# Pooled attention and a gated MLP on one core: the 288-column operands of four more products are read from two quarters in turn

## The chip, the core and the metric

The kernel runs on one core of a Trainium2 chip. The core's engines are TensorE (PE, with its weight loads shown apart as PEld), VectorE (DVE), ScalarE (ACT), GpSimd (POOL) and SyncE (SP), which issues nearly all DMA transfers here. The metric is the device time of one execution in microseconds, taken as the median of several runs. A trace of one further execution, with start and duration of every instruction, is what the rows below are read from.

## The reference

For 8 batches of 576 positions, 8 heads of 64, all fp32:

```python
k_p = k.reshape(B, H, Sp, 8, D).mean(axis=3)         # pooled by 8: Sp = 72
v_p = v.reshape(B, H, Sp, 8, D).mean(axis=3)
attn = softmax(q @ k_p.T / sqrt(D))
x = (attn @ v_p), heads side by side                 # (B, 576, 512)
h = gelu_tanh(x @ w_in)                              # w_in 512 x 1024
u, v = h[..., :512], h[..., 512:]
v_n = (v - mean(v)) / sqrt(var(v) + 1e-6) * g_ln
v_s = einsum('ts,bsd->btd', w_sg, v_n) + b_sg[None, :, None]   # w_sg 576 x 576
out = x + (u * v_s) @ w_out                          # w_out 512 x 512
```

## The kernel before

The program is a long list of small steps. `ORDER`, a list written out in the code, says which step of which batch comes next (`H0+2` is step H, part 0, two batches on), and a last loop pins the order on every engine to it, so each engine works through a fixed queue. Eight batches are interleaved in this way; a batch takes some 60 us.

Most products are "rounded": an fp32 operand is split into a high part that is rounded to fp32r and a low part with the remainder (`wih` and `wil`, `xhl` with both parts of x, `wsh`/`wsl`, `vhh`/`vhl`, `ghi`/`glo`, `woh`/`wol`, `vbh`/`vbl`, `ah`/`al`), and three fp32r matmuls (high by high, high by low, low by high) stand for one fp32 product. The positions (576) lie along the free dimension, in SBUF as one row of 576 floats in a partition. [...] 

The steps that matter here, each for one of four blocks of 128 output rows (features):

- **V**: attention weights times pooled values, x of one block. From batch 3 on (`BY_HEAD` holds 0, 1, 2) it is a rounded product of 8 matmuls per block, 288 columns each, read from `ah`, `al` and `lt`. For batches 0 to 2 it is plain fp32 on 64-wide tiles. Then PSUM is read back three times: `h` (rounded high part into `xhl`), `x` (plain copy into `x32`) and `rest` (the low part). Which engine does each of these is set by the table `OTHER`; `rest` reads PSUM on VectorE, or else `x32` on GpSimd.
- **H** (and **J**, its form for batch 0): the v half of h, positions on the partitions, 512 features as columns, 12 matmuls of 512 columns for each block of positions. Here the moving operand is already read through `woven`: column 0 from the first half, column 1 from the second, column 2 from the first again.
- **U**: the u half of h, 24 matmuls of 288 columns for each block; ScalarE reads PSUM through the gelu into `u`.
- **W**: the product with w_sg, 28 matmuls of 288 columns for each block; VectorE scales by `g_ln` and adds `b_sg` (`bbc`) in PSUM, then multiplies by `u`.
- **O**: the product with w_out, 24 matmuls of 288 columns for each block; VectorE adds it to `x32`.
- **S**, **T**, **D**, **K**, **P**: scores and softmax, transposes, dummy matmuls at the start, and pooling. They issue fp32 matmuls, which the trace shows as two records each.

`woven` is `x.rearrange("p (a b) -> p b a", a=2)`: of n columns, the first and the second half in turn. All matmuls are issued by the helper `mm` (L143).

Of the kernel before, what the change touches and what calls it, by code (L numbers as in the profile page):

```python
# [13 lines left out]
AF = mybir.ActivationFunctionType  # L14
ALU = mybir.AluOpType
AX = mybir.AxisListType

P = 128
# [6 lines left out]
BY_HEAD = (0, 1, 2)  # L25
# [70 lines left out]
def tile_pooled_attn_gmlp(ctx: ExitStack, tc: tile.TileContext, q, k0, kv0, v0, k, v, vleft, w_in, w_sg, bg, w_out, out):  # L96
    nc = tc.nc
    B, _, _, S = q.shape
# [7 lines left out]
    KC = DM // P  # L106
    NT = -(-S // P)
    TAIL = S - (NT - 1) * P
    HALF = S // 2
# [26 lines left out]
    def atile():  # L136
        return ring(psa, [P, 2, NB], "aps", 2)

    def woven(x):
        return x.rearrange("p (a b) -> p b a", a=2)  # L140

    def mm(o, lhsT, rhs, start, stop):
        nc.tensor.matmul(o, lhsT, rhs, start=start, stop=stop)  # L143

# [35 lines left out]
    vbh = const.tile([P, G, P], F32R, name="vbh")  # L180
    vbl = const.tile([P, G, P], F32R, name="vbl")
# [23 lines left out]
    st = {}  # L205
# [9 lines left out]
    def copy(o, i, key):  # L215
        if key in OTHER:
            nc.vector.tensor_copy(o, i)
        else:
            nc.scalar.copy(o, i)  # L219
# [9 lines left out]

    def rest(lo, x, ps, hi, key):  # L230
        if key in OTHER:
            nc.vector.tensor_tensor(lo.rearrange("p (a n) -> p a n", a=2), ps,
                                    hi.rearrange("p (a n) -> p a n", a=2), op=ALU.subtract)
        else:
            nc.gpsimd.tensor_tensor(lo, x, hi, op=ALU.subtract)  # L235

# [357 lines left out]
    def step_V(b, g):  # L594
        ah, al = st.pop(("a", b, g))
        lt, vl = st.get(("lt", b, g // 2)), st.get(("vl", b))
        gl = 2 * (g % 2)
        ps = atile()
        for n in range(2):
            sl = slice(HALF * n, HALF * (n + 1))  # L600
            o = ps[:, n, 0:HALF]
            if b in BY_HEAD:
                for h, (w, x) in enumerate(((st["vp", b][0:SP, g], ah), (st["vo", b][:, g], al))):
                    mm(o[D * h:D * h + D], w, x[:, sl], True, True)
                continue
            mm(o, vbh[:, g], ah[:, sl], True, False)
            mm(o, vbl[:, g], ah[:, sl], False, False)
            mm(o, vl[:, g // 2, gl:gl + 2], lt[:, sl], False, False)
            mm(o, vbh[:, g], al[:, sl], False, True)
        yield  # L610
        if ("x32", b) not in st:
            st["x32", b] = dbl.tile([P, KC, S], F32, name="x32")
            st["xhl", b] = (per.tile([P, 2, KC, S], F32R, name="xhl", tag="xhl"),
                            per.tile([P, KC, 2, TAIL], F32R, name="xta"))
        x32, (xhl, xta) = st["x32", b][:, g], st["xhl", b]
        xs, hi = ps[:, :, 0:HALF], xhl[:, 0, g].rearrange("p (a n) -> p a n", a=2)
        copy(hi, xs, f"h{min(b, 3)}{g}")
        copy(x32.rearrange("p (a n) -> p a n", a=2), xs, f"x{min(b, 3)}{g}")
        yield
        rest(xhl[:, 1, g], x32, xs, xhl[:, 0, g].bitcast(F32), f"V{min(b, 3)}{g}")  # L620
        yield
        move(xta[:, g], xhl[:, :, g, S - TAIL:S].bitcast(F32), f"X{min(b, 3)}{g}")
# [72 lines left out]
    def halves(ps, pairs, first, last):  # L695
        for j, (w, x) in enumerate(pairs):
            for n in range(2):
                mm(ps[:, n, 0:HALF], w, x[:, HALF * n:HALF * (n + 1)], first and j == 0, last and j == len(pairs) - 1)

    def step_U(b, d):  # L700
        xhl = st["xhl", b][0]
        xhi, xlo = xhl[:, 0], xhl[:, 1]
        ps = mtile()
        sl = slice(d * P, (d + 1) * P)
        for c in range(KC):
            halves(ps, [(wih[:, c, sl], xhi[:, c]), (wih[:, c, sl], xlo[:, c]), (wil[:, c, sl], xhi[:, c])],
                   c == 0, c == KC - 1)
        yield
        u = per.tile([P, 2, HALF], F32, name="u", tag=f"u{d}")
        ready(AF.Gelu_apprx_tanh)  # L710
        nc.scalar.activation(u, ps[:, :, 0:HALF], AF.Gelu_apprx_tanh)
        st["u", b, d] = u

    def step_W(b, d):
        vhh, vhl, vht = st["vh", b]
        ps = mtile()
        sl = slice(d * P, (d + 1) * P)
        for c in range(NT - 1):
            halves(ps, [(vhh[:, c, sl], wsh[:, c]), (vhh[:, c, sl], wsl[:, c]), (vhl[:, c, sl], wsh[:, c])],
                   c == 0, False)  # L720
        halves(ps, [(vht[:, sl], wth), (vht[:, sl], wtl)], False, True)
        yield
        u = st.pop(("u", b, d))
        vs = ps[:, :, 0:HALF]
        nc.vector.scalar_tensor_tensor(vs, vs, gcol[:, d:d + 1],  # L725
                                       bbc.rearrange("p (a n) -> p a n", a=2), op0=ALU.mult, op1=ALU.add)
        nc.vector.tensor_tensor(u, vs, u, op=ALU.mult)
        yield
        if ("g", b) not in st:
            st["g", b] = (per.tile([P, KC, S], F32R, name="ghi", tag="ghi"),  # L730
                          per.tile([P, KC, S], F32R, name="glo", tag="glo"))
        ghi, glo = st["g", b]
        uf = u.rearrange("p a n -> p (a n)")
        copy(ghi[:, d], uf, f"G{min(b, 2)}{d}")
        yield
        combine(glo[:, d], uf, ghi[:, d].bitcast(F32), ALU.subtract, f"W{min(b, 2)}{d}")

    def step_O(b, m):
        ghi, glo = st["g", b]
        sl = slice(m * P, (m + 1) * P)  # L740
        x = st["x32", b][:, m].rearrange("p (a n) -> p a n", a=2)
        if b == B - 1 and m == G - 1:
            for n in range(2):
                t = slice(HALF * n, HALF * (n + 1))
                ps = (atile, mtile)[n]()[:, 0, 0:HALF]
                for c in range(KC):
                    for j, (w, z) in enumerate([(woh, ghi), (wol, ghi), (woh, glo)]):
                        mm(ps, w[:, c, sl], z[:, c, t], c == 0 and j == 0, c == KC - 1 and j == 2)
                yield
                nc.vector.tensor_tensor(x[:, n], ps, x[:, n], op=ALU.add)  # L750
                yield
            return
        ps = atile() if b == B - 1 and m % 2 else mtile()

        def part(cs):
            for c in cs:
                halves(ps, [(woh[:, c, sl], ghi[:, c]), (wol[:, c, sl], ghi[:, c]), (woh[:, c, sl], glo[:, c])],
                       c == 0, c == KC - 1)
        part(range(KC - 1))
        yield  # L760
        part([KC - 1])
        yield
        nc.vector.tensor_tensor(x, ps[:, :, 0:HALF], x, op=ALU.add)

    def step_Z(b, m):
        x = st["x32", b][:, m]
# [42 lines left out]
    last = {}  # L809
# [11 lines left out]
def _laid_out(inputs):  # L821

    import numpy as np

    a = {n: np.asarray(x) for n, x in inputs.items()}
    B, H, S, D = a["q"].shape
    G, SP, NT = H // 2, S // POOL, -(-S // P)
    q = a["q"].reshape(B, G, 2, S, D).transpose(0, 1, 2, 4, 3).reshape(B, G, 2 * D, S)
    at = [128 * min(r, 2) + 160 * max(r - 2, 0) + 32 * i + j
          for i in range(NT) for r in range(2 * (i == NT - 1), 4) for j in range(32)]  # L830
    a["q"] = np.stack([q[b] if b == 0 else q[b][:, :, at] for b in range(B)])
    n = P * (S // P)
    run = [t for lo, hi in ((0, 384), (448, 576), (384, 448)) for t in range(lo, hi)]
    kt = a["k"][0].reshape(G, 2, S, D).transpose(2, 0, 1, 3).reshape(S, G, 2 * D)[run]
    vt = a["v"][0].reshape(G, 2, S, D).transpose(2, 1, 0, 3).reshape(S, H * D)[run]
    a["k0"] = kt[:n].reshape(S // P, P, G, 2 * D).transpose(1, 2, 0, 3)
    a["v0"] = vt[:n].reshape(S // P, P, H * D).transpose(1, 0, 2)
    a["kv0"] = np.concatenate([kt[n:].reshape(S - n, H * D), vt[n:]])
    a["k"] = a["k"][1:].reshape(B - 1, G, 2, SP, POOL, D).transpose(0, 2, 5, 1, 3, 4).reshape(B - 1, 2 * D, G, SP, POOL)
    v = a["v"][1:].reshape(B - 1, G, 2 * SP, POOL, D).transpose(0, 1, 2, 4, 3)  # L840
    a["v"] = v[:, :, 0:P].transpose(0, 2, 1, 3, 4)
    a["vleft"] = v[:, :, P:].reshape(B - 1, G * (2 * SP - P), D, POOL)
    w = a["moe_w_in"]
    half = w.shape[1] // 2
    a["moe_w_in"] = np.concatenate([w[:, :half], w[:, half::2], w[:, half + 1::2]], axis=1)
    a["moe_w_sg"] = np.concatenate([a["moe_w_sg"].T, a["moe_w_sg"].T[n:]])
    a["bg"] = np.concatenate([np.broadcast_to(a["moe_b_sg"], (P, S)), a["moe_g_ln"].reshape(-1, P).T], axis=1)
    return a


# [19 lines left out]
```

## Time and profile before

| | |
|---|---|
| Time, median of 3 runs | 528.98 us (528.08 to 529.0) |
| The profiled execution's own time | 528.84 us |
| Its span, first to last instruction | 527.1 us |
| PE busy | 517.7 us, 98% of the span |
| DVE busy | 376.2 us, 71% |
| ACT busy | 258.3 us, 49% |
| POOL busy | 240.7 us, 46% |
| Granted TensorE clock, mean over the span | 0.999 of full speed |

Busy times are sums of instruction durations without overlap. A matmul's row has a duration that runs on behind the start of the next one, so the time that a matmul costs the engine is read from the distance between starts, not from its duration.

### The profile page before, as it was taken

Reading aid. Unit: us, or ns where it says so; the run is one execution under the profiler, and the core shown is the slowest. Engines: PE = TensorE matmul, PEld = TensorE weight load, DVE = VectorE, ACT = ScalarE, POOL = GpSimd, SP = SyncE. Lnnn points to the kernel's source line nnn. Section 1 sums busy time; section 2 is a strip of 40 time slices with the busy share of each in tenths; the row PEclk is TensorE's granted clock in tenths of the full one; section 3 lists DMA queues with packets and bytes.
Section 4 is the critical chain, followed back from the end, with each engine's and each line's share of the span. In section 5 each row is a group of like instructions: output and inputs, shape, how many; then the busy total and the mean of one; then the engine's idle time right before and its main releaser. Section 6 shows DMA issues by size and latency. Waiting matters only on the chain.

```text
span 527.1 us, 9508 instructions
## 1 busy us (share of the span) xinstructions
PE 517.7 (98%) x3594; PEld 489.9 (93%) x3594; DVE 376.2 (71%) x593; ACT 258.3 (49%) x510; POOL 240.7 (46%) x333
## 2 busy tenths in 40 slices
PE   8889999999999999999999999999999999999997
PEld 8658899899989999999999999999999999999997
DVE  1789999668857886887679769877749765642362
ACT  2888871586336554485703577274253743142000
POOL 4797664553455629183335615754134741261010
PEclk9999999999999999999999999999999999999999
DMA  8995125837461563056432632344431224000002
GB/s 282 406 347 188 59 68 124 238 110 231 109 176 67 158 224 93 24 153 197 148 98 79 180 96 88 112 110 111 151 125 24 90 68 114 24 22 24 24 2 112
DMA packets 42810, 66.64 MB, mean 126 GB/s; under 512 B 5532, under 2 KB 22028, under 8 KB 42764
## 3 DMA queue, kind: packets, MB, share of 16 engines
q1 hardware_dynamic: 42476, 65.59, 40.6%
q8 instruction: 28, 0.46, 0.4%
q10 hardware_dynamic: 288, 0.44, 0.2%
q14 instruction: 18, 0.15, 0.1%
HBM read 47.14 MB, written 18.73 MB: 125 GB/s over the span
## 4 chain that ended last, share of the span: by engine, by line
PE 92%; ACT 3%; DVE 2%; POOL 2%; issue 0%; POOLq 0%; ACTq 0%
PE mps L143 77%; PE aps L143 15%; ACT e L472 1%; POOL e L458 1%; DVE nmax L506 0%; PE aps L190 0%; POOL rstd L482 0%; DVE e L463 0%; ACT vg L491 0%; DVE glo L228 0%; ACT e L468 0%; POOL glo L228 0%; ACT ah L219 0%; ACT L212 0%; ACT vhh L219 0%
## 5 line engine op out<-in xcount | busy, mean ns | idle before, releaser
L143 PE MATMUL mps<-xhl,wih 128*128 128x288 f32 x512 | 88.7, 295 | 0.3 <-ACT vg L671 0.3
L143 PE MATMUL mps<-wih,xhl 128*128 128x512 f32 x256 | 77.7, 383 | 0.0
L143 PEld LDWEIGHTS mps<-xhl,wih 128*128 128x128 f32 x512 | 75.2, 188 | 1.3 <-ACT vg L671 0.5
L458 POOL TENSOR_TENSOR e<-e,ssum 128x720 f32<-128x720 f32 x29 | 42.1, 1455 | 58.4 <-DVE ssum L457 49.0
L235 POOL TENSOR_TENSOR xhl<-x,xhl 128x576 fp32r<-128x576 f32 x22 | 31.3, 1433 | 53.4 <-ACT x L219 34.2
L143 PE MATMUL mps<-wsh,vhh 128*128 128x288 f32 x256 | 54.8, 295 | 0.0
L143 PE MATMUL mps<-wsl,vhh 128*128 128x288 f32 x256 | 54.7, 295 | 0.0
L143 PE MATMUL mps<-wsh,vhl 128*128 128x288 f32 x256 | 54.7, 295 | 0.0
L143 PE MATMUL mps<-xhl,wil 128*128 128x288 f32 x256 | 54.6, 294 | 0.0
L143 PEld LDWEIGHTS mps<-wih,xhl 128*128 128x128 f32 x256 | 48.1, 189 | 6.4
L143 PE MATMUL mps<-ghi,woh 128*128 128x288 f32 x244 | 53.2, 298 | 0.0
L143 PE MATMUL mps<-glo,woh 128*128 128x288 f32 x244 | 52.4, 294 | 0.0
L143 PE MATMUL mps<-ghi,wol 128*128 128x288 f32 x244 | 52.3, 294 | 0.0
L725 DVE SCALAR_TENSOR_TENSOR mps<-mps,both 128x576 f32<-128x576 f32 x32 | 26.1, 814 | 34.8 <-PE mps L143 34.4
L143 PE MATMUL mps<-wil,xhl 128*128 128x512 f32 x128 | 46.5, 379 | 0.0
L481 POOL TENSOR_TENSOR rstd<-mv,eps 128x1 f32<-128x1 f32 (+1 forms) x40 | 10.3, 258 | 76.8 <-DVE mv L676 76.5
L228 POOL TENSOR_TENSOR glo<-u,ghi 128x576 fp32r<-128x576 f32 x18 | 25.7, 1428 | 41.3 <-ACT ghi L219 23.9
L143 PE MATMUL aps<-kbd,qT 128*128 128x144 f32 x300 | 41.7, 288 | 1.9 <-ACT ah L219 1.2
L143 PEld LDWEIGHTS aps<-kbd,qT 128*128 128x128 f32 x300 | 39.0, 190 | 4.8 <-ACT ah L219 1.4
L143 PEld LDWEIGHTS mps<-wsh,vhh 128*128 128x128 f32 x256 | 41.1, 188 | 0.4 <-issue 0.4
L143 PEld LDWEIGHTS mps<-wsh,vhl 128*128 128x128 f32 x256 | 41.1, 188 | 0.2 <-DVE vhl L228 0.2
L143 PEld LDWEIGHTS mps<-xhl,wil 128*128 128x128 f32 x256 | 40.9, 188 | 0.0
(182 smaller groups left out, 1236.0 us busy)
## 6 DMA issues: line engine op xcount, KB each, us to landing
qT<-in_q SPq DMA_DIRECT2D x31, 288.0 KB
out<-x SPq DMA_DIRECT2D x31, 288.0 KB
kraw<-in_k SPq DMA_DIRECT2D x14, 576.0 KB
vraw<-in_v SPq DMA_DIRECT2D x14, 512.0 KB
al<-tfar SPq DMA_DIRECT2D x20, 288.0 KB
tfar<-y SPq DMA_DIRECT2D x56, 80.0 KB
raw<-in_moe_w_in SPq DMA_DIRECT2D x4, 1024.0 KB
tfar<-y SPq DMA_DIRECT2D x56, 64.0 KB
```

The source lines that it names most:

```text
L143: nc.tensor.matmul(o, lhsT, rhs, start=start, stop=stop)
L228: (nc.vector if key in OTHER else nc.gpsimd).tensor_tensor(o, x, y, op=op)
L235: nc.gpsimd.tensor_tensor(lo, x, hi, op=ALU.subtract)
L458: (nc.gpsimd if key in OTHER else nc.vector).tensor_tensor(e, e, rec.unsqueeze(3).broadcast_to([P, NT, 2, SP]), op=ALU.mult)
L472: nc.scalar.activation(e[:, i, h], slots[i][:, h], AF.Exp, bias=nmax[:, i, h:h + 1], accum_out=ssum[:, i, h:h + 1])
L481: nc.gpsimd.tensor_tensor(rstd, var, eps[:n, 1:2], op=ALU.add)
L725: nc.vector.scalar_tensor_tensor(vs, vs, gcol[:, d:d + 1], bbc.rearrange("p (a n) -> p a n", a=2), op0=ALU.mult, op1=ALU.add)
```

## The change

In U, W, O and the rounded V, each matmul's moving operand of 288 columns goes through `woven`: column 0 comes from the first quarter (144 floats) of its half row, column 1 from the second quarter, column 2 from the first again. The two places lie 144 floats, 576 bytes, apart. PSUM then holds the positions in that turned order. Where a result leaves PSUM it is read through `seen`, which takes every second column first and then the others, so that everything in SBUF stays in the order it had. Operations that read PSUM for batches 0 to 2 in V get the same four-dimensional form with the columns in plain order. `b_sg` is added in PSUM, so its copy is put into the turned order on the host. No instruction is added, removed or moved on any engine: both programs list the same instructions with the same shapes in the same order.

```diff
+    def seen(ps):
+        return ps.rearrange("p n (b a) -> p n a b", a=2)
+
+    def quarters(x):
+        return x.rearrange("p (n a b) -> p n a b", n=2, a=2)
...
     def rest(lo, x, ps, hi, key):
         if key in OTHER:
-            nc.vector.tensor_tensor(lo.rearrange("p (a n) -> p a n", a=2), ps,
-                                    hi.rearrange("p (a n) -> p a n", a=2), op=ALU.subtract)
+            nc.vector.tensor_tensor(quarters(lo), ps, quarters(hi), op=ALU.subtract)
         else:
             nc.gpsimd.tensor_tensor(lo, x, hi, op=ALU.subtract)
...
-            mm(o, vbh[:, g], ah[:, sl], True, False)
-            mm(o, vbl[:, g], ah[:, sl], False, False)
-            mm(o, vl[:, g // 2, gl:gl + 2], lt[:, sl], False, False)
-            mm(o, vbh[:, g], al[:, sl], False, True)
+            mm(o, vbh[:, g], woven(ah[:, sl]), True, False)
+            mm(o, vbl[:, g], woven(ah[:, sl]), False, False)
+            mm(o, vl[:, g // 2, gl:gl + 2], woven(lt[:, sl]), False, False)
+            mm(o, vbh[:, g], woven(al[:, sl]), False, True)
...
-        xs, hi = ps[:, :, 0:HALF], xhl[:, 0, g].rearrange("p (a n) -> p a n", a=2)
-        copy(hi, xs, f"h{min(b, 3)}{g}")
-        copy(x32.rearrange("p (a n) -> p a n", a=2), xs, f"x{min(b, 3)}{g}")
+        xs = ps[:, :, 0:HALF]
+        xs = xs.rearrange("p n (a b) -> p n a b", a=2) if b in BY_HEAD else seen(xs)
+        copy(quarters(xhl[:, 0, g]), xs, f"h{min(b, 3)}{g}")
+        copy(quarters(x32), xs, f"x{min(b, 3)}{g}")
...
     def halves(ps, pairs, first, last):
         for j, (w, x) in enumerate(pairs):
             for n in range(2):
-                mm(ps[:, n, 0:HALF], w, x[:, HALF * n:HALF * (n + 1)], first and j == 0, last and j == len(pairs) - 1)
+                mm(ps[:, n, 0:HALF], w, woven(x[:, HALF * n:HALF * (n + 1)]), first and j == 0,
+                   last and j == len(pairs) - 1)
...
-        nc.scalar.activation(u, ps[:, :, 0:HALF], AF.Gelu_apprx_tanh)
+        nc.scalar.activation(u.rearrange("p n (a b) -> p n a b", a=2), seen(ps[:, :, 0:HALF]), AF.Gelu_apprx_tanh)
...
-        nc.vector.tensor_tensor(u, vs, u, op=ALU.mult)
+        un = u.rearrange("p n (a b) -> p n a b", a=2)
+        nc.vector.tensor_tensor(un, seen(vs), un, op=ALU.mult)
...
-        x = st["x32", b][:, m].rearrange("p (a n) -> p a n", a=2)
+        x = quarters(st["x32", b][:, m])
...
-        nc.vector.tensor_tensor(x, ps[:, :, 0:HALF], x, op=ALU.add)
+        nc.vector.tensor_tensor(x, seen(ps[:, :, 0:HALF]), x, op=ALU.add)
...
+    turned = a["moe_b_sg"].reshape(2, 2, S // 4).transpose(0, 2, 1).reshape(S)
+    a["bg"] = np.concatenate([np.broadcast_to(turned, (P, S)), a["moe_g_ln"].reshape(-1, P).T], axis=1)
```

The last block of O in the last batch has a form of its own, with one half after the other; it is changed in the same way.

## Rows read from the trace of the kernel before

**Rows 1.** The page: busy us (share of the span) x instructions; tenths in 40 slices.

```profile
PE 517.7 (98%) x3594; PEld 489.9 (93%) x3594; DVE 376.2 (71%) x593; ACT 258.3 (49%) x510; POOL 240.7 (46%) x333
...
PE   8889999999999999999999999999999999999997
...
DVE  1789999668857886887679769877749765642362
...
PEclk9999999999999999999999999999999999999999
```

**Rows 2.** Waits of PE: who waited for whom, us in total, times, longest.

```profile
PE aps L143 <- POOL ident masks.py:199: 1.4, 1, 1.4
PE aps L190 <- DVE xhl L232: 1.2, 1, 1.2
PE aps L143 <- ACT ah L219: 1.2, 1, 1.2
PE aps L190 <- POOL e L458: 0.7, 1, 0.7
```

**Rows 3.** Chain that ended last: start us, us, what, with the number of instructions.

```profile
111.81 5.18 PE mps L143 x24
...
309.58 1.23 PE aps L143 x10
310.81 3.17 PE mps L143 x24
313.98 1.06 PE aps L143 x8
315.04 6.34 PE mps L143 x48
321.38 1.08 PE aps L143 x8
322.46 7.39 PE mps L143 x56
```

**Rows 4.** PE by shape: instructions, busy us, mean ns of one, idle before them.

```profile
L143 PE MATMUL mps<-wih,xhl 128*128 128x512 f32 x256 | 77.7, 383 | 0.0
...
L143 PE MATMUL aps<-kbd,qT 128*128 128x144 f32 x300 | 41.7, 288 | 1.9 <-ACT ah L219 1.2 <-PE mps L143 0.4 <-ACT kbd L383 0.3
```

**Rows 5.** Weight loads of the page: instructions, busy us, mean ns, idle before.

```profile
L143 PEld LDWEIGHTS mps<-wih,xhl 128*128 128x128 f32 x256 | 48.1, 189 | 6.4
...
L143 PEld LDWEIGHTS aps<-kbd,qT 128*128 128x128 f32 x300 | 39.0, 190 | 4.8 <-ACT ah L219 1.4
L143 PEld LDWEIGHTS mps<-wsh,vhh 128*128 128x128 f32 x256 | 41.1, 188 | 0.4 <-issue 0.4
```

**Rows 6.** DVE and ACT by shape, those that read PSUM's 576 columns or 288.

```profile
L727 DVE TENSOR_TENSOR u<-mps,u 128x576 f32<-128x576 f32 x32 | 24.2, 757 | 1.1
L763 DVE TENSOR_TENSOR x<-mps,x 128x576 f32<-128x576 f32 x30 | 22.4, 746 | 24.8 <-PE mps L143 24.7
...
L750 DVE TENSOR_TENSOR x<-mps,x 128x288 f32<-128x288 f32 x1 | 0.5, 458 | 1.1 <-PE mps L143 1.1
...
L711 ACT ACTIVATE u<-mps 128x576 f32<-128x576 f32 x32 | 20.7, 649 | 32.2 <-PE mps L143 32.0
...
L671 ACT ACTIVATE vg<-mps 128x512 f32<-128x512 f32 x32 | 18.8, 595 | 38.5 <-PE mps L143 38.4
```

**Rows 7.** ACT by shape: contiguous 512 floats, and every second word from SBUF.

```profile
L219 ACT CAST vhh<-vg 128x512 fp32r<-128x512 f32 x22 | 13.6, 616 | 0.7 <-DVE vg L487 0.3
...
L279 ACT ACTIVATE top<-raw 128x512 f32<-128x512 f32 x12 | 8.6, 718 | 3.7 <-DMA raw<-in_moe_w_in 1.9 <-POOL wil L228 1.7
```

**Rows 8.** Timeline of DVE around 472 us: start us, us, instruction.

```profile
471.89 0.72 DVE L763 TENSOR_TENSOR x<-mps,x 128x576 f32<-128x576 f32 x1
```

**Rows 9.** Timeline of PE at the same place.

```profile
472.45 0.43 PE L143 MATMUL mps<-glo,woh 128*128 128x288 f32 x2
472.71 0.49 PE L143 MATMUL mps<-ghi,woh 128*128 128x288 f32 x2
```

**Rows 10.** Windows: us, busy (x) of PE, PEld, DVE, ACT, POOL; clock; DMA.

```profile
0.00:56.00 56.00, 50.33 (x308) 41.28 (x309) 37.92 (x63) 39.99 (x100) 39.13 (x61) 1.00 0.86 301
56.00:119.00 63.00, 62.93 (x442) 58.17 (x441) 52.25 (x81) 38.86 (x112) 37.44 (x47) 1.00 0.42 114
```

More of the change, by code (lines that the diff above doesn't have):

```diff
@@ L747, in step_O @@
                     for j, (w, z) in enumerate([(woh, ghi), (wol, ghi), (woh, glo)]):
-                        mm(ps, w[:, c, sl], z[:, c, t], c == 0 and j == 0, c == KC - 1 and j == 2)
+                        mm(ps, w[:, c, sl], woven(z[:, c, t]), c == 0 and j == 0, c == KC - 1 and j == 2)
                 yield
-                nc.vector.tensor_tensor(x[:, n], ps, x[:, n], op=ALU.add)
+                nc.vector.tensor_tensor(x[:, n], ps.rearrange("p (b a) -> p a b", a=2), x[:, n], op=ALU.add)
                 yield
@@ L846, in _laid_out @@
     a["moe_w_sg"] = np.concatenate([a["moe_w_sg"].T, a["moe_w_sg"].T[n:]])
-    a["bg"] = np.concatenate([np.broadcast_to(a["moe_b_sg"], (P, S)), a["moe_g_ln"].reshape(-1, P).T], axis=1)
+    turned = a["moe_b_sg"].reshape(2, 2, S // 4).transpose(0, 2, 1).reshape(S)
+    a["bg"] = np.concatenate([np.broadcast_to(turned, (P, S)), a["moe_g_ln"].reshape(-1, P).T], axis=1)
     return a
```

## The prediction

> **What bounds the kernel now.** I read the page first. TensorE is busy for 517.7 of 527.1 us, at a granted clock of full speed in every slice, and no other engine passes 71% [rows 1]. So TensorE sets the time, unless it waits for others inside the span. It hardly does: the longest of its waits is 1.4 us [rows 2], it idles for 527.1 - 517.7 = 9.4 us in all, and 56 - 50.33 = 5.7 us of that lie in the first 56 us, where the first loads and the dummy matmuls are [rows 10]. What is left is how long TensorE takes for a matmul, and that must come from distances between starts. The chain that ended last shows them best, since its pieces are unbroken runs of matmuls with a count [rows 3]. At 310.81 us, 24 matmuls of a U block take 3.17 us, 132.1 ns each; the next 48 take 6.34 us, again 132.1; two W blocks take 7.39 us for 56, 132.0; the eight of V take 1.06 us, 132.5. These read 288 columns contiguously. At 111.81 us stand 24 matmuls of H, of 512 columns that are read from two halves in turn: 5.18 us, 215.8 ns each.
>
> [...] The two kinds differ in two things: length, and the order of reading. The change alters only the second.
>
> [...] The fp32 products of S have 144 columns and a weight load of the same 128x128 [rows 4, 5]; ten of their records take 1.23 us, 123 ns each [rows 3]. [...] This says that a short matmul with a full weight load isn't held at 132 ns by loading or issue as such: weight loads last 188 to 190 ns in all three kinds [rows 5]. [...]
>
> [...]
>
> **The change, part by part.**
>
> Matmuls. U has 32 blocks x 24, W 32 x 28, O 32 x 24, V 20 x 8: 768 + 896 + 768 + 160 = 2592 matmuls. Read in turn, I give each 120.0 + 2.5 = 122.5 ns, the fixed part being H's. Scaling H's rate per column instead (215.8 x 288 / 512) gives 121.4. Against 132.1 that saves 9.6 to 10.7 ns each, 24.9 to 27.7 us. I take 24.9. The other end for this unknown is a saving of nothing.
>
> Reading PSUM back with every second column. In SBUF the data stay as they were, so only instructions that read PSUM through `seen` can change: on VectorE 32 products of W, 33 additions of O, and in V from batch 3 on, by the table, 5 each of `h`, `x` and `rest`, together 80; on ScalarE 32 gelus, 15 `h` and 15 `x`, together 62. VectorE takes 746 ns for 576 columns and 458 for 288, so 1.0 ns a column; ScalarE 649 for 576 and 595 for 512, 0.84 ns a column [rows 6]. No row reads PSUM at a step of two. The nearest does so in SBUF: ScalarE takes 718 ns for every second word of 512 against 616 for 512 contiguous ones, another operation too [rows 7]. By that a step of two costs 0.1 us at most for an instruction, 62 x 0.1 = 6 us on ScalarE, which idles for half the span, and 8 us on VectorE. Bound from above: half rate, which adds 576 ns on VectorE and 0.48 us on ScalarE to each, 46 and 30 us of busy time in all. Below nothing I don't go: each element is still fetched once. I take no cost, since the row with a step of two is far nearer to the same time than to twice. The four-dimensional form for batches 0 to 2 reads the same addresses in the same order and costs nothing; the turned bias is host work.
>
> What is late next. TensorE gains on the others: 10 ns a matmul is 0.23 us for each block of U or O and 0.27 for W. Where a result was just in time, TensorE will now wait. One such place: O's addition ends at 471.89 + 0.72 = 472.61 [rows 8], and the matmuls that take over its PSUM tile start at 472.71 [rows 9], 0.10 us later. TensorE comes there one block of O (0.23 us) sooner relative to the matmul that let the addition start, so about 0.13 us come back. Behind that matmul the whole PE queue stands, in the fixed order; but VectorE, whose work waits for PE, loses nothing more. I take 2 such places for each of 8 batches, 2 us in all as an estimate; the bounds are 0 and 7. A general shortage isn't in sight: VectorE's fullest batch is 52.25 of 63 us [rows 10]; if that batch shrinks by 3 us, it is 87%.
>
> Sum: the profiled execution took 528.84 us, 1.7 more than its span, which this doesn't touch. 528.84 - 24.9 + 2.0 = 505.9, **506 us**. It lies 0.14 us below the median of the runs shown, which makes no difference here. A difference of 0.2% (1 us) is about what a measurement of this kernel can tell from none.
>
> **The rivals.**
>
> (a) Partial. Two quarters 576 bytes apart needn't behave like two halves 1024 apart; half of the excess gone would be 12.5 us, 516. Or reading back at half rate: VectorE then has 376 + 46 = 422 us to do in 506, 83%, and every U, W and O block's tile comes free 0.5 to 0.6 us later. With 96 blocks, and a tenth to a fifth of the added 0.55 us not covered by the other tile of the ring, that gives 5 to 11 us back: 511 to 517. For it: no row shows either. Against it: rows 7. [...]
>
> (b) Nothing. The 132 ns is a floor of short fp32r matmuls, by their weight load or else; the order of reading doesn't matter: 528.8. For it: no short fp32r matmul below 132 ns stands in the trace. Against it: the 123 ns of the fp32 records with the same weight loads.
>
> [...]
>
> **How the numbers follow.** Forecast, every 288-column matmul at 121 to 124 ns and 0 to 7 us of new waits, 501 to 512 us: 0.68. (a), 510 to 525: 0.15. (b): 0.07. (c): 0.10. The likeliest gives 506. The range runs from 501.1 (27.7 saved, no waits) to 518, which takes in the forecast and nearly all of (a), and leaves out some 0.18 at the upper side. Faster by over 0.2%: 0.68 + 0.15 = 0.83; same 0.07; slower 0.10.
>
> **What would show it.** In the chain, a U or O block of 24 should take 2.94 us in place of 3.17, two W blocks 6.86 in place of 7.39, with H's 24 still at 5.18. If U stays at 3.17 us, (b); if O or U differ from W, the place in memory matters and not the order alone. The reading back: `u<-mps` on VectorE still near 757 ns and on ScalarE near 649, `x<-mps` near 746. If these stand near 1.3 us, it is (a). PE's waits should grow by 2 us, behind `x<-mps`, `u<-mps` and the low parts `glo`. The prediction is wrong if PE's distances stay, or if they fall and the waits take more than 7 us.

## The result

The changed kernel takes 512.78 us (median of 4 runs, 510.75 to 513.77) against 528.99 us for the kernel before beside it. The ratio is 0.9684, 95% interval 0.964 to 0.9727, so 3.2% faster. The profiled execution took 510.75 us, with a span of 509.0 us against 527.1. Two of the four runs had a mean granted clock of 0.992 and 0.993 and were some 2 us longer than the other two, as some later runs of the kernel before were too, so spans are compared below from executions at a clock of 0.999 or 1.0, unless the text says otherwise. Single spans still differ by 1 us and more: the changed kernel's second such execution has 510.2, and 28 of the kernel before lie between 526.3 and 528.0, with a mean of 526.9.

The page of the changed kernel, to be held against [rows 1]: busy us (share) x instructions.

```profile
PE 495.6 (97%) x3594; PEld 464.9 (91%) x3594; DVE 380.5 (75%) x593; ACT 258.3 (51%) x510; POOL 239.1 (47%) x333
```

TensorE is busy for 22 us less and still for 97% of the span. The chain that ended last, over a stretch of U, V and W like that of [rows 3], of another batch, and at two blocks of H (start us, us, what, number of instructions):

```profile
186.83 5.88 PE mps L149 x48
192.71 0.99 PE aps L149 x8
193.70 6.86 PE mps L149 x56
...
389.61 5.18 PE mps L149 x24
```

48 matmuls of U in 5.88 us and 56 of W in 6.86 us are 122.5 ns each, the forecast to its last digit; V's eight take 0.99 us, 123.8 ns. H's 24 stay at 5.18 us, and O's pairs start 0.245 us apart in the timeline further down. The reading back, which answers to [rows 6] (DVE and ACT by shape: busy us, mean ns of one, idle before):

```profile
L735 DVE TENSOR_TENSOR u<-mps,u 128x576 f32<-128x576 f32 x32 | 24.2, 757 | 1.1
L771 DVE TENSOR_TENSOR x<-mps,x 128x576 f32<-128x576 f32 x30 | 22.3, 743 | 18.3 <-PE mps L149 18.0
...
L718 ACT ACTIVATE u<-mps 128x576 f32<-128x576 f32 x32 | 20.6, 648 | 26.2 <-PE mps L149 26.1
```

757, 743 and 648 ns against 757, 746 and 649: a step of two in PSUM costs VectorE and ScalarE nothing. So 24.9 us came off the matmuls, yet the span fell by 527.1 - 509.0 = 18.1 us. The other 6.8 us were given back, where the prediction had 2; by the means of the spans, 526.9 and 509.6, it is 7.6. The chain that ended last shows where to look. These are its shares of the span, before and now:

```profile
PE 92%; ACT 3%; DVE 2%; POOL 2%; issue 0%; POOLq 0%; ACTq 0%
```

```profile
PE 65%; DVE 14%; POOL 8%; ACT 7%; DMA 3%; issue 2%; SPq 1%; POOLq 0%; DVEq 0%; ACTq 0%
```

TensorE is nearly as full as before by its busy share, but a third of this chain now runs through other engines. TensorE's waits, to be held against [rows 2] (us in total, times, longest):

```profile
PE aps L149 <- POOL ident masks.py:199: 1.4, 1, 1.4
PE aps L196 <- DVE xhl L238: 1.2, 1, 1.2
PE aps L149 <- ACT ah L225: 1.1, 1, 1.1
PE aps L149 <- ACT kbd L388: 1.0, 1, 1.0
PE mps L149 <- DVE vhl L234: 0.8, 2, 0.6
PE aps L196 <- POOL e L463: 0.7, 1, 0.7
PE mps L149 <- DVE x L771: 0.5, 2, 0.3
PE mps L149 <- DVE vg L671: 0.4, 1, 0.4
```

The first three, and that for `e`, stood there before. New, or longer, are the waits for `kbd` on ScalarE and for `vhl`, `x` and `vg` on VectorE; smaller ones, for `u` on both engines, for `al` and for the load of q, stand further down in the view. The largest is at 288 us. PE's timeline there, from O's first pair after H (start us, us, instruction, idle before and its releaser):

```profile
278.67 0.41 PE L149 MATMUL mps<-ghi,woh 128*128 128x288 f32 x2
...
287.00 0.41 PE L149 MATMUL mps<-ghi,wol 128*128 128x288 f32 x2
287.25 0.41 PE L149 MATMUL mps<-glo,woh 128*128 128x288 f32 x2
288.64 0.64 PE L149 MATMUL aps<-kbd,qT 128*128 128x144 f32 x3 [0.98 <-ACT kbd L388]
```

and ScalarE's:

```profile
278.87 0.60 ACT L677 ACTIVATE vg<-mps 128x512 f32<-128x512 f32 x1 [2.43 <-PE mps L149]
...
285.16 1.28 ACT L218 ACT_TABLE_LOAD   x1
...
286.56 1.48 ACT L473 ACTIVATE e<-e 128x720 f32<-128x720 f32 x2
287.95 1.31 ACT L388 ACTIVATE kbd<-kp 64x144 f32<-64x144 f32 x4
```

The same place in the kernel before, first PE, then ScalarE:

```profile
295.48 0.42 PE L143 MATMUL mps<-glo,woh 128*128 128x288 f32 x2
296.23 0.51 PE L143 MATMUL aps<-kbd,qT 128*128 128x144 f32 x2 [0.33 <-ACT kbd L383]
```

```profile
286.44 0.60 ACT L671 ACTIVATE vg<-mps 128x512 f32<-128x512 f32 x1 [2.43 <-PE mps L143]
...
295.53 1.32 ACT L383 ACTIVATE kbd<-kp 64x144 f32<-64x144 f32 x4
```

The scaling of k (`kbd`) stands behind a table load and two exponentials. ScalarE's stretch from the reading of `vg` to `kbd` takes as long as it did: 278.87 to 287.95 is 9.08 us, 286.44 to 295.53 was 9.09. Beside it TensorE works off 72 matmuls of O, which take 8.83 us in place of some 9.5 (72 x 132 ns). So TensorE comes 0.7 us earlier to a result that was 0.49 us late already (296.23 against a due start of 295.74), and is now 1.14 us late. Of the 1.14 us between the due start (287.50) and 288.64 the waits view counts 0.98: a matmul's row goes on behind the next one's start, and the first 0.16 us of this wait hide under it. A wait costs something after it, too, as a place further on shows:

```profile
316.03 0.41 PE L149 MATMUL mps<-wsl,vhh 128*128 128x288 f32 x2
316.65 0.51 PE L149 MATMUL mps<-wsh,vhl 128*128 128x288 f32 x2 [0.21 <-DVE vhl L234]
317.00 0.41 PE L149 MATMUL mps<-wth,vht 128*128 128x288 f32 x2
```

Pairs start 0.245 us apart; here the gap is 0.62 us, so 0.37 of wait where the view shows 0.21, and the pair after it takes 0.35 us, 0.10 more than it should.

With these two shares most of the 6.8 us can be added up from the starts of TensorE's matmuls. From 56 us on the waits view counts ten waits in the changed kernel, 3.9 us, and one in the kernel before, 0.3. Taken as late starts, with the pair behind each, the ten are 6.7 us over the matmuls' bare distances (122.5 or 132.1 ns for 288 columns, 215.8 for 512, the median of its kind for any other) and the one is 0.6. So nine new waits and a longer one make 6.1 of the 6.8 us. Late starts too short for the view add 1.3 us, and 0.6 us less is lost in the first 56 us.

### The profile page after: what moved, and what is told of

Its sections match the earlier page's. It is cut to its first block, busy times and chain, and to the rows that moved or that the text cites. A ratio compares the mean times of both kernels' runs of the same rounds, so it can differ in the third digit from the quotient of the medians.

```text
span 509.0 us, 9508 instructions
## 1 busy us (share of the span) xinstructions
PE 495.6 (97%) x3594; PEld 464.9 (91%) x3594; DVE 380.5 (75%) x593; ACT 258.3 (51%) x510; POOL 239.1 (47%) x333
## 4 chain that ended last, share of the span: by engine, by line
PE 65%; DVE 14%; POOL 8%; ACT 7%; DMA 3%; issue 2%; SPq 1%; POOLq 0%; DVEq 0%; ACTq 0%
PE mps L149 54%; PE aps L149 10%; POOL e L463 2%; POOL rstd L487 1%; DVE ssum L482 1%; DMA qT<-in_q 1%; DVE bst L681 1%; POOL glo L234 1%; SPq L243 1%; DMA kraw<-in_k 1%; ACT L218 1%; DVE y L537 1%; DVE nmax L511 1%; ACT vg L496 1%; DVE vhl L234 1%
## 5 line engine op out<-in xcount | busy, mean ns | idle before, releaser
L149 PE MATMUL mps<-xhl,wih 128*128 128x288 f32 x512 | 84.1, 287 | 1.1 <-DVE vg L671 0.4
L149 PEld LDWEIGHTS mps<-xhl,wih 128*128 128x128 f32 x512 | 71.7, 189 | 2.4 <-ACT u L718 0.9
L463 POOL TENSOR_TENSOR e<-e,ssum 128x720 f32<-128x720 f32 x29 | 41.9, 1446 | 56.3 <-DVE ssum L462 51.5
L149 PE MATMUL mps<-wsh,vhl 128*128 128x288 f32 x256 | 52.5, 287 | 0.8 <-DVE vhl L234 0.8
L149 PE MATMUL mps<-wsh,vhh 128*128 128x288 f32 x256 | 52.7, 288 | 0.1
L149 PE MATMUL mps<-xhl,wil 128*128 128x288 f32 x256 | 52.3, 286 | 0.0
L149 PE MATMUL mps<-wsl,vhh 128*128 128x288 f32 x256 | 52.3, 286 | 0.0
L149 PE MATMUL mps<-ghi,woh 128*128 128x288 f32 x244 | 51.2, 290 | 0.6 <-DVE u L735 0.3
L149 PE MATMUL mps<-glo,woh 128*128 128x288 f32 x244 | 50.3, 287 | 0.0
L149 PE MATMUL mps<-ghi,wol 128*128 128x288 f32 x244 | 50.2, 286 | 0.0
L149 PEld LDWEIGHTS mps<-ghi,woh 128*128 128x128 f32 x244 | 38.5, 189 | 2.6 <-issue 1.4
## 6 DMA issues: line engine op xcount, KB each, us to landing
vraw<-in_v SPq DMA_DIRECT2D x14, 512.0 KB
```

The lines of the kernel that those rows point to most:

```text
L463: (nc.gpsimd if key in OTHER else nc.vector).tensor_tensor(e, e, rec.unsqueeze(3).broadcast_to([P, NT, 2, SP]), op=ALU.mult)
```

## The experiments

Two questions were open: what about the order of reading gives the 9.6 ns, and where the 6.8 us went. Times of one group stand beside runs of the kernel before on the same chip.

**How the columns are read.** Four kernels change only the order in which a moving operand is read. In turn, the changed kernel's U (5.88 us for 48 matmuls of 288 columns) and H (5.18 us for 24 of 512) give, taken as a line over the columns, 0.417 ns a column and 2.5 ns a matmul; a tick, here and in the expectation, is that 0.417 ns.

H and J in a row:

```diff
-                    mm(o, xhl[:, x, c, t], woven(w[:, c, DF2:2 * DF2]), c == 0 and w is wih and x == 0, c == KC - 1 and w is wil)
+                    mm(o, xhl[:, x, c, t], w[:, c, DF2:2 * DF2], c == 0 and w is wih and x == 0, c == KC - 1 and w is wil)
...
-                mm(o, xhi[:, c, t], woven(wih[:, c, sl]), c == 0, False)
+                mm(o, xhi[:, c, t], wih[:, c, sl], c == 0, False)
...
-    a["moe_w_in"] = np.concatenate([w[:, :half], w[:, half::2], w[:, half + 1::2]], axis=1)
+    a["moe_w_in"] = w
```

> As the changed kernel, but H and J read their 512 columns in a row instead of from two halves in turn (the weights' columns are laid out for it on the host). Theory: reading in a row at one column per tick costs extra, and turning removes it. If that extra is a fixed 9.6 ns per matmul, H's distance goes from 215.8 to 225.4 ns, 448 matmuls, +4.3 us. If it grows with the columns, 9.6 x 512/288 = 17.1 ns, distance 232.9 ns, +7.7 us. Rival: the order alone is not it, short matmuls are: 215.8 ns stays and the time is that of the changed kernel, 512.8 us. Some of the added time can be taken up by TensorE's waits, up to 3 us.

515.75 us (514.22 to 516.15), ratio to before 0.9733 (0.9697 to 0.9769), span 513.8. The chain, 24 of H's matmuls:

```profile
392.73 5.60 PE mps L149 x24
```

5.60 / 24 = 233 ns, the second of the three answers. What is over the 2.5 ns is 0.451 ns a column for 512 columns in a row and 0.450 for 288 in a row: both pay 1.08 ticks a column, in turn both pay 1.00. So it is a rate, not a cost of short matmuls. Of 448 x 17.5 = 7.8 us the span shows 4.8; the gaps between TensorE's starts, which are 3 us smaller than in the changed kernel, took up the rest.

Every second float:

```diff
+    def turned(x):
+        return x.rearrange("p (b a) -> p a b", a=2)
...
-                mm(ps[:, n, 0:HALF], w, woven(x[:, HALF * n:HALF * (n + 1)]), first and j == 0,
+                mm(ps[:, n, 0:HALF], w, turned(x[:, HALF * n:HALF * (n + 1)]), first and j == 0,
...
```

> As the changed kernel, but the 288 columns are read as every second float (0, 2, 4, ... then 1, 3, 5, ...) and read back accordingly. If it is enough that a column is not the neighbour of the one before it, the distance stays 122.5 ns and the time 511 to 514 us. If two separate places in turn are needed, the distance goes back to 132 ns or more and the time to 528 us or more. [...]

850.88 us, ratio 1.6062 (1.601 to 1.6115). The trace is of an execution with a granted clock of 0.556; the time is that of executions at 0.999. The chain of the trace, 24 of H's matmuls and 48 of U's:

```profile
187.80 9.26 PE mps L152 x24
...
334.55 12.32 PE mps L152 x48
```

H's stand 386 ns apart, 1.79 times the 215.8 of full clock, U's 257 ns. At 0.999 the distance is worked out from the times, against the next kernel below, whose chain is TensorE's to 95% and holds hardly any wait: 153.3 + (850.9 - 582.1) / 2592 = 257 ns, 2.12 ticks a column. So this order takes the same 257 ns at either clock, and what holds it back isn't TensorE's clock.

Four eighths in turn:

```diff
+    def turned(x):
+        return x.rearrange("p (a b) -> p b a", a=4)
...
     def seen(ps):
-        return ps.rearrange("p n (b a) -> p n a b", a=2)
+        return ps.rearrange("p n (b a) -> p n a b", a=4)
...
```

> As the changed kernel, but from four eighths of the row in turn (72 floats, 288 bytes apart) instead of two quarters; read back at a step of four. If two places in turn are what helps, four do so too: 122.5 ns, 511 to 514 us, unless the step of four makes the reading back longer (VectorE's product of W is 757 ns now). If four open places are too many, the distance is over 132 ns and the time over 528 us.

582.13 us, ratio 1.0994 (1.0963 to 1.1024). The chain, and VectorE's reading at a step of four:

```profile
405.42 7.36 PE mps L152 x48
...
438.57 5.18 PE mps L152 x24
```

```profile
L738 DVE TENSOR_TENSOR u<-mps,u 128x576 f32<-128x576 f32 x32 | 24.2, 757 | 1.1
```

153.3 ns, 1.26 ticks a column, while H beside it stays at 215.8 ns. The reading back is unchanged even at a step of four.

Pairs in turn:

```diff
+    def turned(x):
+        return x.rearrange("p (a b c) -> p b a c", a=2, c=2)
...
```

> As the changed kernel, but two neighbours from the first quarter, then two from the second, and so on; the reading back is left as it is, so positions come out in another order than the reference's. If it is each neighbour in succession that costs, about half of the 9.6 ns comes back: 127 ns, some 520 us. If a change of place every few columns is enough, 122.5 ns and 511 to 514 us.

665.5 us, ratio 1.2573 (1.2532 to 1.2615).

```profile
458.14 8.88 PE mps L152 x48
```

185.0 ns, 1.52 ticks a column, far above both answers. My idea that it is enough not to read neighbours in succession fell with these three: two places in turn, one column each, is the fastest order of the five (1.00), in a row comes next (1.08), then four in turn (1.26), pairs (1.52) and every second float (2.12). I have no mechanism that gives these five numbers.

**Only the reading back.** The matmuls read in a row again, `seen` stays:

```diff
-                mm(ps[:, n, 0:HALF], w, woven(x[:, HALF * n:HALF * (n + 1)]), first and j == 0,
+                mm(ps[:, n, 0:HALF], w, x[:, HALF * n:HALF * (n + 1)], first and j == 0,
...
```

> The changed kernel with the matmuls reading in a row again, and only the reading back at a step of two left (positions come out in another order than the reference's). If the step of two costs nothing, W's product stays at 757 ns, O's addition at 743 to 746, the gelu at 648, and the time is that of the kernel before, 528 to 530 us. If reading at a step of two is slower, these durations rise, and the time with them.

One run, at a clock of 1.0: 528.28 us, span 526.6, as the kernel before.

```profile
371.71 6.34 PE mps L149 x48
```

```profile
L735 DVE TENSOR_TENSOR u<-mps,u 128x576 f32<-128x576 f32 x32 | 24.2, 757 | 1.1
L771 DVE TENSOR_TENSOR x<-mps,x 128x576 f32<-128x576 f32 x30 | 22.4, 745 | 25.1 <-PE mps L149 25.0
```

```profile
L718 ACT ACTIVATE u<-mps 128x576 f32<-128x576 f32 x32 | 20.6, 648 | 32.5 <-PE mps L149 32.4
```

The two halves of the change are apart: the reading back costs nothing, the matmuls give all.

**Where the 6.8 us went, by moving work.** Eight entries of the order list, at six places (two of which are shown):

```diff
-S1+3 H3+1 K1+3 H4+1 H4+1 U0+1 T0+2 C0+4 H4+1 T1+2
+S1+3 H3+1 H4+1 H4+1 U0+1 T0+2 C0+4 H4+1 K1+3 T1+2
...
-H0+4 S2+5 S2+5 O1+3 B0+6 E0+6 H2+4 O1+3 S3+5 S3+5 Z0+3 O2+3 O2+3 V1+4 S3+5 K0+6 S0+6 S0+6 Z1+3 S1+6 B1+6 O3+3 K1+6 O3+3
+H0+4 K0+6 K1+6 S2+5 S2+5 O1+3 B0+6 E0+6 H2+4 O1+3 S3+5 S3+5 Z0+3 O2+3 O2+3 V1+4 S3+5 S0+6 S0+6 Z1+3 S1+6 B1+6 O3+3 O3+3
```

> The changed kernel with eight entries of the order list moved, so that at six places, of some 330 ns to 1.15 us of wait each, what TensorE waits for is issued earlier on its engine (kbd before two exponentials, the additions of O before a sum or a statistic, a low part of v before a softmax sum, the pooling of k behind two additions). Theory: the 6 to 7 us that the faster matmuls gave back are waits for results that used to come just in time, queued behind other work on VectorE and ScalarE. Then these waits, about 3 us with their restarts, go: span 505 to 507 us against 509.0, time 2 to 4 us below the changed kernel's. Rival: what is given back is TensorE's own (restarts, clock) or comes from a general shortage of VectorE; then a wait only moves and the span stays at 508 to 510 us.

512.0 us (511.22 to 512.51), ratio 0.9669 (0.9646 to 0.9691); span 510.0, none of the 2 to 4 us. The waits:

```profile
PE mps L150 <- DVE x L772: 1.8, 2, 1.3
...
PE aps L150 <- DMA qT<-in_q: 1.1, 2, 0.6
PE aps L150 <- DVE al L597: 0.8, 1, 0.8
```

Those for `kbd` and `vg` are gone; in their place stand longer ones for `x`, `al` and the load of q. The wait had only moved, as the rival said. The same list for the kernel before:

> The kernel before, matmuls reading in a row, with the same eight entries moved. By the theory these results were in time there, so nothing is gained: 528 to 530 us, span 526 to 528. If the order list just was bad at these places, it gains 2 to 3 us here as well.

530.09 us (10 runs), ratio 1.0026 (1.0007 to 1.0046): the list is no better there either, a quarter of a per cent worse. Then the three places that seemed clean, and a fourth, `kbd` ahead of the exponentials as above, with an addition of O put before the softmax sum that waits for them:

> The changed kernel with four of the eight entries moved, at the three places where the wait went and no longer one took its place close by: the pooling of k behind the addition of H4 (123 us), O's addition before a softmax sum (94 us) and before a statistic (458 us). These waits are 0.6, 0.36 and 0.25 us. If each is only a matter of its own queue, the span falls by 1.2 to 1.6 us to about 507.6. If waits move on to the next late result, as the eight entries together showed, the span stays at 508.5 to 510.

> As the three places, and at 288 us also the scaling of k before two exponentials, now with the softmax sum that waits for them put behind O's addition (with the eight entries, O's addition stood behind that sum, and TensorE waited 1.5 us for it). If that clears the place, another 1.0 to 1.2 us: span 506 to 507. If the delay goes on with the softmax, to the transposes of the next batch, 508 to 510.

511.78 us (508.86 to 512.46), ratio 0.9667 (0.9642 to 0.9692), span 510.5; and 512.14 us (510.83 to 514.18), ratio 0.9686 (0.9662 to 0.9711), span 511.1 in an execution whose clock was 0.997. Neither is told from the changed kernel. The spread is too wide to exclude a gain of 1 us: two of the five runs with three places moved, at 508.86 and 509.58 us, are about as short as was expected. A clearly better order was not found.

**By taking work away.** Half of the reading back of W and O:

```diff
-        nc.vector.tensor_tensor(un, seen(vs), un, op=ALU.mult)
+        nc.vector.tensor_tensor(un[:, 0], seen(vs)[:, 0], un[:, 0], op=ALU.mult)
...
-        nc.vector.tensor_tensor(x, seen(ps[:, :, 0:HALF]), x, op=ALU.add)
+        nc.vector.tensor_tensor(x[:, 0], seen(ps[:, :, 0:HALF])[:, 0], x[:, 0], op=ALU.add)
```

> The changed kernel, in which W's product with u and O's addition handle only the first 288 of the 576 columns (the rest of the result is left out). VectorE has 18 to 19 us less to do, all of it in reading back. Theory of results that come just late: the waits behind them (O's addition, W's product, and what queues behind these on VectorE) go, TensorE's time over its bare distances falls by 2 to 3 us, span 506 to 507. Rival, waits come from DMA, ScalarE and GpSimd: under 1 us, span 508 to 509.

510.32 us, ratio 0.9637 (0.9612 to 0.9662), span 507.4, 1.6 us less; a second execution at a clock of 1.0 has 509.0, so this alone is hardly more than the spread, and it lies between the two answers. The waits view no longer has a wait for `x` or `vg`, while that for `kbd` stays at 1.0 us.

Half of the softmax division:

```diff
         (nc.gpsimd if key in OTHER else nc.vector).tensor_tensor(
-            e, e, rec.unsqueeze(3).broadcast_to([P, NT, 2, SP]), op=ALU.mult)
+            e[:, :, 0], e[:, :, 0], rec[:, :, 0].unsqueeze(2).broadcast_to([P, NT, SP]), op=ALU.mult)
```

> The changed kernel, in which the division of the softmax handles one of the two heads alone (the other stays unnormalized). GpSimd has some 20 us less to do, VectorE a little. If what was given back hangs on VectorE and ScalarE at the places named, the waits behind vhl, kbd, x, vg and u stay and the span is 508 to 509. If GpSimd's part of the softmax chain sets when results come, waits behind al, kbd and x fall together and the span is 505 to 507.

507.39 us, ratio 0.96 (0.9586 to 0.9613), span 505.7, 3.3 us less (505.1 to 506.4 in four executions). GpSimd's division and, beside it, VectorE's `al`, which isn't touched, here and in the changed kernel:

```profile
L463 POOL TENSOR_TENSOR e<-e,ssum 128x360 f32<-128x360 f32 x29 | 24.5, 846 | 57.7 <-DVE ssum L462 53.3 <-DMA tfar<-y 3.7 <-DMA left<-in_vleft 0.4
```

```profile
L596 DVE TENSOR_TENSOR al<-al,ah 128x576 fp32r<-128x576 f32 x20 | 17.0, 852 | 1.1 <-ACT ah L593 1.0
```

```profile
L596 DVE TENSOR_TENSOR al<-al,ah 128x576 fp32r<-128x576 f32 x20 | 18.5, 925 | 1.1 <-ACT ah L593 1.0
```

and TensorE's waits:

```profile
PE mps L149 <- DVE vhl L234: 0.6, 1, 0.6
...
PE aps L149 <- ACT kbd L388: 0.4, 1, 0.4
```

GpSimd is busy for 47% of the span, and yet a shorter instruction on it, 846 ns in place of 1446, shortens waits for `kbd` (0.4 us in place of 1.0) and `vg` on other engines: the division lies in the chain from the scores to the transposes. VectorE's `al` is shorter here too, so this run doesn't part the shorter chain from less hindrance on VectorE. Both together:

> The changed kernel with both takings away: reading back of W and O for the first 288 columns only, and the softmax division for one head only (the rest of the result is left out). Alone the first gave 1.6 us of span, the second 3.3. If the two remove different waits, together 4 to 5 us, span 504 to 505, and nearly all of the 6.8 us that were given back is gone. If they shorten the same chain, the span stays at 505.5 to 506.

505.88 us (505.44 to 508.33), ratio 0.957 (0.9529 to 0.9612). The span is 504.5 us, 4.5 us less than the changed kernel, nearly the sum of 1.6 and 3.3; it leaves 2.3 of the 6.8 us. By the means of the executions at 0.999 or 1.0 the three take 1.4, 3.9 and 5.6 us off, of 7.6. From 56 us on the view has four waits in place of ten, three of them old ones:

```profile
PE mps L149 <- DVE vhl L234: 0.6, 1, 0.6
PE mps L149 <- ACT u L718: 0.4, 1, 0.4
PE aps L149 <- ACT kbd L388: 0.4, 1, 0.4
PE aps L149 <- DVE ssum L462: 0.3, 1, 0.3
```

As late starts they are 3.0 us, against 6.7 in the changed kernel and 0.6 in the kernel before; that for `kbd` is nearly back to what it was there.

## Why the prediction was right, point by point

**What bounds the kernel** held for the kernel before: TensorE, and its time comes from distances between starts. In the changed kernel TensorE has only 65% of the chain that ended last, so it is no longer the only bound. The choice of the order of reading against length held too. H in a row shows it directly: with the same 512 columns the distance went from 215.8 to 233 ns. The saving of 9.6 ns a matmul, which the prediction took, is 8% of a column's time, at both lengths; at 288 columns the two are the same number.

**The matmul term** was 122.5 ns and 24.9 us, and 122.5 it is. Its parts, 120.0 and 2.5 ns, were my estimate, from a time for a column that no run before the result shows; in the changed kernel the distances in turn, 122.5 ns for 288 columns and 215.8 for 512, give 0.417 ns a column, 120.0 for 288, and 2.5 beside it. The other value, 121.4 by scaling, is out.

**The reading back** at no cost held at 757, 743 and 648 ns in the changed kernel and at 757, 745 and 648 alone. That part of rival (a) is out.

**New waits** is the term that was mis-sized: 2.0 us, with bounds of 0 and 7, against 6.8 us. Three things were wrong in its working. It counted only the lead that TensorE gains over one block (0.23 us), and only where a result came within 0.1 us before. At 288 us TensorE gains 0.7 us, over 72 matmuls, on a stretch of ScalarE that keeps its 9.1 us. And a wait costs more than its lateness: 0.10 us behind it, as the restart at 316 us shows. "VectorE loses nothing more" was wrong as well: a chain on ScalarE, VectorE and GpSimd keeps its length when TensorE's stretch beside it shrinks. The place worked out in the prediction, at 472.71 us, shows the size. It stands at 457.98 us now:

```profile
457.48 0.41 PE L149 MATMUL mps<-glo,woh 128*128 128x288 f32 x2
457.98 0.51 PE L149 MATMUL mps<-ghi,woh 128*128 128x288 f32 x2
```

0.50 us lie between starts in place of 0.245, and the pair after it starts at 458.33, another 0.10 late: 0.35 us where 0.13 was put.

That these 6.8 us are waits for other engines' work, and not TensorE's own, is shown twice: 6.1 of them stand as late starts at places where the profile names what came late, and the last three experiments take away half of two kinds of instruction, without a change on TensorE, and 4.5 us go with them. Three lists of another order gave nothing that stands out of the spread, and the first of them only moved the waits. What is left in the last kernel is named in the profile (`vhl`, `u`, `ssum`), but nothing was tried on it alone.

**The time** fell in the range partly by luck. The forecast's own line, 501 to 512, is missed by the median of 512.78 and met by the two executions at full clock, 510.75 and 511.95; the range reached up to 518 for rival (a), and what took the time there was neither of its mechanisms. The sign of being wrong, waits of more than 7 us, is just not met by the profiled executions (6.8) and just met by the means (7.6).

**The rivals.** (b) is out by the distances. (c), slower, is out: two places in turn gave 122.5 ns in place of 132.1 in a row (288 columns, 576 bytes apart), and 215.8 in place of 233 (512 columns, 1024 bytes apart). (a) came out in its size, 6.8 us given back, by waits, but not by either of its mechanisms.

## What to carry to other kernels

Where a rounded product's moving operand is read in a row at full clock, expect 0.45 ns a column plus 2.5 ns, as here at 288 and 512 columns (132.1 and 233 ns); two places in turn, one column each, gave 0.417 plus 2.5 (122.5 and 215.8 ns), and no other order should be taken without a measurement, since the three others tried here were 16 to 95% slower than reading in a row. The permutation was undone for nothing where VectorE and ScalarE read fp32 from PSUM (757, 743 and 648 ns against 757, 746 and 649). When the bound engine gets 5% faster in a fixed schedule, some of the gain comes back as short waits, a quarter of it in this kernel; to size it, set each stretch of TensorE that shrinks against the chain that runs beside it. Here the cure lay in work taken off the other engines' chains, more than in single places of the order.

## What the runs showed that I had not expected

The spread of the orders: 122.5, 132, 153, 185 and about 257 ns for the same 288 columns, with at most the reading back changed beside it. The last is the same at a clock of 0.556, in the trace, and of 0.999, worked out from the times.

A wait of TensorE shows 0.16 us short at the two places above, since it starts under the row of the matmul before, and costs some 0.10 us more after it. So ten waits of 3.9 us in the view are 6.7 us of time.

VectorE's `al` took 829 ns on average in the kernel before, 925 in the changed one and 852 with half of the division on GpSimd, though its work is the same. In the changed kernel the five longest took 0.88 to 1.83 us, all beside GpSimd's division or its low part of x, the other fifteen 0.70 to 0.76 us, four of them beside other GpSimd work. That some of GpSimd's instructions hold VectorE up is likely from this, but no run was made for it alone.
